# Windowed attention and a token/channel mixer in one kernel: mask added on TensorE and scores on 64 rows for batch 0, token weight permuted on chip, batch 1's first loads put ahead of the second channel weight

## The chip, the cores and the metric

The kernel runs on one core of one Trainium2 chip. The metric is the time of one execution in microseconds on the device; shown is the median of three runs. A profile of one more execution gives a trace of every instruction and every DMA packet; its own time is given beside its span below.

A core has five engines that run their own instruction streams: PE (TensorE, matrix products), DVE (VectorE), ACT (ScalarE), POOL (GpSimd) and SP (which here only issues DMAs). They meet through semaphores. PE multiplies a stationary operand by a moving one and writes to a bank of PSUM, from which DVE or ACT must copy the result to SBUF.

## The reference

Eight batches, eight heads, sequence 576, head width 64. Attention with a window: heads 0 to 3 see the last 32 positions ("plain"), heads 4 to 7 every fourth of the last 128 ("dilated").

```python
rel = pos[:, None] - pos[None, :]
mask_plain = (rel >= 0) & (rel < 32)
mask_dil = (rel >= 0) & (rel < 128) & (rel % 4 == 0)
scores = np.where(mask, q @ k.T / 8, -1e9)
x = softmax(scores) @ v                       # heads side by side: x is (8, 576, 512)
h = relu(x.T @ w_tok1) @ w_tok2               # tokens: 576 -> 256 -> 576
u = x + h.T
out = u + relu(u @ w_ch1) @ w_ch2             # channels: 512 -> 1536 -> 512
```

Inputs and output are float32; the kernel computes in float16 with float32 accumulation.

## The kernel before

**A batch's stages.** Loads (q, k, v in float32), casts to float16, transposes of q and k on PE, scores, values, token mixing (h1, then u, then the transposed uT), and the channel stage `gen_main` (gp with the weight w3, then yp with w4).

**Heads go in pairs**, hp 0 to 3. Positions are held for the dilated pairs by residue modulo 4 (r = 0 to 3), so that a dilated window becomes a plain band over every fourth position. `transposes(b, nm, hp)` (L245) transposes one pair's q or k: four blocks of 128 positions and the last 64 (the tail). k is copied by DVE into `kt` (L261). q is copied by ACT into `qz` twice, once for each head: 64 rows hold the head, the other 64 rows hold zeros (L266, L268), so that a score matmul runs over all 128 rows with the zeros removing the other head.

**Scores.** `scores_plain` (L273) makes per head three blocks of 160 queries in one PSUM bank, exponentiates them on ACT (L284), and then does the fourth block and the tail of both heads in one small bank (L290 to L301). `scores_dil` (L309) makes four blocks of 128 per head, and a small bank for both tails. The mask is a product after the exponential: two multiplications per pair (L303, L304, L328, L329), on DVE for batch 0 and on POOL for the other batches (`mask_engine`, L270). Scores are not shifted by their maximum. The tag "sc" has two banks, "fl" three, "main" three: eight in all.

**Values.** `values(b, h)` (L332) multiplies the weights by v with a column of ones appended, takes the reciprocal of the sum (L362) and scales into `xn` (through the helper at L106), both on DVE.

**Mixing.** `emit_h1` (L365) makes one half (heads 0 to 3, heads 4 to 7) of one of two blocks of 128 hidden units, with a relu on ACT. The first half needs w_tok1 with its rows in natural order (`w1n`), the second half by residue (`w1p`); both are loaded by their own DMA. `emit_u` (L376) makes the five row tiles of u and adds x on DVE (L386, L396). `emit_uT` (L398) transposes u.

**Order of the work.** The order on each engine is the order of the program's text. For batch 0 up to the channel stage the order is written out by hand (L596 to L623, with `warm(n)`, which gives PE n products on zeros to do). From then on `interleave` (L514) mixes the channel stage of batch b with `steps` for later batches: each step has a due time on a scale of PE microseconds from the stage's start, and the channel stage is asked for its next piece whenever no step is due. Steps that are left when the channel stage runs out follow at once.

**Loads.** SP's queue carries q, k, v and the outputs; in batch 0 ACT's queue carries k. POOL's queue carries the constants and the weights, with a cast from float32 to float16 on the way: w1n, w1p, w1t, w2, four pieces of w3, three pieces of w4 (L563 to L577), between its casts of batch 0. Buffers of the raw loads exist once, so a load waits until the batch before has been cast. `gate(t, src)` (L553) is a copy of one element on POOL from a weight to a load's buffer, so that this load waits for that weight. L626 holds all loads of batch 1 until the last piece of w3 has landed.

Of the kernel before, what the change touches and what calls it, by code (L numbers as in the profile page):

```python
# [68 lines left out]
def kernel(  # L69
# [44 lines left out]
    dtail = const[:, 384 + BLK:CW].rearrange("p (x y c) -> p x y c", x=1, y=2)  # L114
    const_np = np.concatenate(
# [22 lines left out]
    def emit_fixed():  # L138
        nc.gpsimd.memset(idle, 0.0)
        for hp in range(4):  # L140
            nc.vector.memset(qz[hp][64:128, 0], 0.0)
            nc.vector.memset(qz[hp][0:64, 1], 0.0)
            nc.vector.memset(kt[hp][:, S:640], 0.0)
# [96 lines left out]
    xn, u16, u16t, uT, gt = {}, {}, {}, {}, {}  # L240
# [4 lines left out]
    def transposes(b, nm, hp):  # L245
# [14 lines left out]
        if nm == "k":  # L260
            nc.vector.tensor_copy(out=natural(kt[hp][:, 0:S]), in_=got)  # L261
            return
        for h in range(2):
# [6 lines left out]
    def mask_engine(b):  # L270
        return nc.vector if b == 0 else nc.gpsimd

    def scores_plain(b, hp):  # L273
# [3 lines left out]
        mid = None  # L277
        for h in range(2):
            p = bank("sc", 2, f"sc_{b}_{hp}_{h}")
            for kb in range(3):  # L280
                nc.tensor.matmul(  # L281
                    out=p[:, BLK * kb:BLK * kb + BLK], lhsT=kt[hp][:, 128 * kb:128 * kb + 128],
                    rhs=qz[hp][:, h, 128 * kb:128 * kb + BLK], start=True, stop=True)
# [4 lines left out]
        p = bank("sc", 2, f"sm_{b}_{hp}")  # L288
        for h in range(2):
            nc.tensor.matmul(  # L290
                out=p[:, BLK * h:BLK * h + BLK], lhsT=kt[hp][:, 384:512],
                rhs=qz[hp][:, h, 384:384 + BLK], start=True, stop=True)
        for h in range(2):
            nc.tensor.matmul(
                out=p[:, 320 + 64 * h:384 + 64 * h], lhsT=kt[hp][:, 512:640],
                rhs=qz[hp][:, h, 512:S], start=True, stop=True)
        nc.scalar.activation(  # L297
            out=blocks[:, :, 3, 0:BLK], in_=p[:, 0:320].rearrange("p (h c) -> p h c", c=BLK),
            func=AF.Exp, scale=0.125)
        nc.scalar.activation(  # L300
            out=tl, in_=p[:, 320:448].rearrange("p (h c) -> p h c", c=64), func=AF.Exp, scale=0.125)  # L301
        eng = mask_engine(b)
        mult(eng, blocks[:, :, :, 0:BLK], blocks[:, :, :, 0:BLK], band)  # L303
        mult(eng, tl, tl, band[:, 0, :, 0:64])  # L304
        yield 0.21

    def scores_dil(b, hp):
        a = attd[hp - 2]
        diag = a[:, :, 0:DTL].rearrange("p h (r c) -> p h r c", c=128)  # L309
        tl = a[:, :, DTL + 64:DTL + 320].rearrange("p h (x c) -> p h x c", c=128)[:, :, :, 0:64]  # L310
        for h in range(2):
            p = bank("sc", 2, f"sc_{b}_{hp}_{h}")
            for r in range(4):
                nc.tensor.matmul(  # L314
                    out=p[:, 128 * r:128 * r + 128], lhsT=kt[hp][:, r:512:4],
                    rhs=qz[hp][:, h, 128 * r:128 * r + 128], start=True, stop=True)
            nc.scalar.activation(out=a[:, h, 0:DTL], in_=p, func=AF.Exp, scale=0.125)  # L317
            yield 0.22
        p = bank("sc", 2, f"sm_{b}_{hp}")
        for h in range(2):  # L320
            for x, keys in enumerate((kt[hp][:, 384:512], kt[hp][:, 512:640])):
                nc.tensor.matmul(out=p[:, 128 * h + 64 * x:128 * h + 64 * x + 64], lhsT=keys,
                                 rhs=qz[hp][:, h, 512:S], start=True, stop=True)
        nc.scalar.activation(
            out=tl, in_=p[:, 0:256].rearrange("p (h x c) -> p h x c", x=2, c=64),
            func=AF.Exp, scale=0.125)
        eng = mask_engine(b)
        mult(eng, diag, diag, band[:, :, :, 0:128])  # L328
        mult(eng, tl, tl, dtail)  # L329
        yield 0.12  # L330

    def values(b, h):  # L332
# [30 lines left out]
        mult(nc.vector, xn[b][:, :, D * h:D * h + D], av[:, :, 0:64], rec)  # L363

    def emit_h1(b, jb, half, t):  # L365
# [8 lines left out]
        relu(nc.scalar, t[:, c], p)  # L374

    def emit_u(b, s, h1):  # L376
        p = bank("fl", 3, f"up_{b}_{s}")
        if s < 4:
            for jb in range(2):
                nc.tensor.matmul(out=p[:, 0:256], lhsT=w2[jb][:, 128 * s:128 * s + 128],  # L380
                                 rhs=h1[jb][:, 0:256], start=(jb == 0), stop=(jb == 1))
            for jb in range(2):
                nc.tensor.matmul(out=p[:, 256:512], lhsT=w2p[jb][:, s],  # L383
                                 rhs=h1[jb][:, 256:512], start=(jb == 0), stop=(jb == 1))
            t = sb.tile([128, DM], FP16, tag="u16", bufs=8, name=f"u16_{b}_{s}")
            nc.vector.tensor_tensor(out=t, in0=p, in1=xn[b][:, s], op=ALU.add)  # L386
# [70 lines left out]
    def gen_main(b):  # L457
# [5 lines left out]
        for mb in range(NMB):  # L463
            t = gt[(b // 2, mb)]
            for sh in range(2):
# [5 lines left out]
                relu(nc.vector if (2 * mb + sh) % 4 == 3 else nc.scalar, t[:, g0 + 288 * sh:g0 + 288 * sh + 288], p[:, 0:288])  # L471
# [85 lines left out]
    cast_qk(0, "k", 0, nc.vector)  # L557
    cast_tails_qk(0, nc.vector)
    for hp in range(1, 4):
        cast_qk(0, "q", hp, nc.gpsimd)  # L560
    for s in range(4):
        cast_vn(0, s, nc.gpsimd)
    nc.gpsimd.dma_start(out=w1n, in_=moe_w_tok1[0:512, :].rearrange("(s p) j -> p s j", p=128))  # L563
    cast_tail_v(0, nc.gpsimd)
    nc.gpsimd.dma_start(out=w1p, in_=moe_w_tok1[0:512, :].rearrange("(m r) j -> m r j", r=4))
    nc.gpsimd.dma_start(out=w1t[0][0:64], in_=moe_w_tok1[512:S, :])
    nc.gpsimd.dma_start(out=w1t[1][64:128], in_=moe_w_tok1[512:S, :])
    nc.gpsimd.dma_start(out=w2a[:, :, 0:S], in_=moe_w_tok2.rearrange("(j p) t -> p j t", p=128))
    cast_vd(0, 0, nc.gpsimd)
# [44 lines left out]
    for h in range(2, 4):  # L614
        va[h]()
        warm(1)
# [76 lines left out]
```

## Time and profile before

| what | value |
|---|---|
| median of 3 runs | 334.49 us (334.07 to 334.78) |
| the profiled execution, its own time | 333.64 us |
| its span (first to last instruction) | 331.86 us |
| granted TensorE clock, mean | 0.994 |
| busy PE / weight load / DVE / ACT / POOL | 300.9 / 253.2 / 154.8 / 173.3 / 155.4 us |
| first channel matmul of batch 0 | 33.33 us |
| first channel matmul of batch 1 | 84.31 us |
| DMA traffic | 43.51 MB, 131 GB/s over the span |

How to read it: the span is cut into 40 slices of 8.3 us; a digit is the busy share of a slice in tenths. A row of instructions gives start, duration, engine, source line, operation, output and input by the program's names, shape and count, and in brackets how long the engine had stood idle just before and what ended that idle time. A row of waits gives who waited for whom, total us, times, and the longest. Rows of groups give busy time and the mean duration of one instruction in nanoseconds.

### The profile page before, as it was taken

What the parts mean: (1) busy time and instruction counts of PE and PEld (TensorE: products, weight loads), DVE (VectorE), ACT (ScalarE), POOL (GpSimd) and SP (SyncE); (2) the same over time, 40 slices, a digit from 0 to 9 for tenths busy, and PEclk for the clock granted to TensorE, in tenths of its full rate; (3) what the DMA queues carried; (4) which work ended last, traced back from release to release, by engine and by line L of the source; (5) the groups of instructions that cost most, each with busy time, mean ns of one, the idle gap of its engine ahead of it and who ended that gap; (6) DMA issues with size and microseconds to landing.
All of it is one profiled execution on the core that took longest, in us unless ns stands there. A gap on an engine that the chain in (4) does not pass through costs nothing.

```text
span 331.9 us, 7976 instructions
## 1 busy us (share of the span) xinstructions
PE 300.9 (91%) x3221; PEld 253.2 (76%) x3221; DVE 154.8 (47%) x329; ACT 173.3 (52%) x380; POOL 155.4 (47%) x211
## 2 busy tenths in 40 slices
PE   5567769999999989998999989998999989999995
PEld 2444547988787878897887888897887888898785
DVE  5676122556366426453545336453545327442222
ACT  2941539589652845548463835548463845522600
POOL 7691066917990499007960499007960490000000
PEclk9999979999999999999999999999999999999999
DMA  8999999948432995920377226921100211002022
GB/s 214 252 162 202 221 270 249 254 129 267 102 100 46 299 228 158 283 70 32 91 241 178 66 65 168 262 81 34 63 3 2 64 65 34 2 32 95 1 65 95
DMA packets 68276, 43.51 MB, mean 131 GB/s; under 512 B 35952, under 2 KB 67056, under 8 KB 68240
## 3 DMA queue, kind: packets, MB, share of 16 engines
q1 hardware_dynamic: 63328, 37.63, 42.5%
q0 software_dynamic: 3312, 4.20, 7.5%
q10 hardware_dynamic: 1600, 1.18, 1.4%
q8 instruction: 25, 0.41, 0.6%
q14 instruction: 11, 0.09, 0.1%
HBM read 37.59 MB, written 9.44 MB: 142 GB/s over the span
## 4 chain that ended last, share of the span: by engine, by line
PE 75%; ACT 11%; DMA 5%; DVE 5%; issue 1%; SPq 1%; POOL 0%; ACTq 0%; POOLq 0%
PE gp L468 27%; PE yp L485 22%; DMA l_q<-in_q_dram 5%; ACT qz L266 4%; PE h1p L373 4%; PE yp L505 3%; ACT attp L284 2%; PE up L380 2%; PE tp_q L253 2%; PE up L383 2%; PE sc L281 2%; ACT qz L268 2%; DVE xn L106 1%; ACT attd L317 1%; PE h1p L371 1%
## 5 line engine op out<-in xcount | busy, mean ns | idle before, releaser
L468 PE MATMUL gp<-uT,w 128*128 128x288 f16 x768 | 110.5, 288 | 1.1 <-ACT gt L100 0.7
L100 ACT ACTIVATE gt<-gp 128x288 f16<-128x288 f32 x144 | 59.1, 412 | 64.9 <-PE gp L468 55.7
L485 PE MATMUL yp<-w,gt 128*128 128x256 f16 x756 | 92.5, 273 | 0.0
L468 PEld LDWEIGHTS <-w 128*128 128x128 f16 x768 | 72.5, 99 | 18.5 <-issue 1.6
L106 POOL TENSOR_TENSOR attp<-attp,const 128x1280 f16<-128x1280 f16 (+1 forms) x28 | 41.8, 1521 | 91.9 <-ACT attp L297 78.5
L485 PEld LDWEIGHTS <-gt 128*128 128x128 f16 x768 | 76.4, 106 | 4.5 <-ACT gt L100 0.3
L495 DVE TENSOR_TENSOR o<-yp,u 128x512 f32<-128x512 f32 x31 | 21.4, 692 | 48.8 <-PE yp L485 48.8
L102 DVE TENSOR_SCALAR gt<-gp 128x288 f16<-128x288 f32 x48 | 21.8, 453 | 38.0 <-PE gp L468 34.8
L106 POOL TENSOR_TENSOR attd<-attd,const 128x1024 f16<-128x1024 f16 (+1 forms) x28 | 38.3, 1398 | 0.0
L261 DVE COPY kt<-tp_k 128x576 f16<-128x576 f16 x32 | 24.1, 754 | 29.5 <-PE tp_k L259 29.4
L106 DVE TENSOR_TENSOR xn<-av,rec 128x320 f16<-128x320 f32 x64 | 31.5, 492 | 2.2
L268 ACT COPY qz<-tp_q 64x576 f16<-64x576 f16 x32 | 20.2, 631 | 15.0 <-PE tp_q L259 14.6
L386 DVE TENSOR_TENSOR u<-up,xn 128x512 f16<-128x512 f32 x32 | 21.4, 686 | 5.5 <-PE up L383 5.3
L317 ACT ACTIVATE attd<-sc 128x512 f16<-128x512 f32 x32 | 17.8, 598 | 11.2 <-PE sc L314 10.9
L94 ACT COPY uT<-tpu 128x576 f16<-128x576 f16 x16 | 10.1, 640 | 25.0 <-PE tpu L417 24.9
L100 ACT ACTIVATE h<-h1p 128x256 f16<-128x256 f32 x32 | 12.3, 384 | 16.5 <-PE h1p L373 15.2
L284 ACT ACTIVATE attp<-sc 128x480 f16<-128x480 f32 x32 | 18.1, 571 | 5.2 <-PE sc L281 3.7
L266 ACT COPY qz<-tp_q 64x576 f16<-64x576 f16 x32 | 20.2, 630 | 0.8 <-PE tp_q L257 0.5
L362 DVE RECIPROCAL rec<-av 128x5 f32<-128x5 f32 x64 | 12.3, 192 | 14.9 <-PE av L349 8.5
L96 POOL CAST c_q<-l_q 128x512 f16<-128x512 f32 x27 | 16.9, 626 | 4.0 <-DMA l_q<-in_q_dram 4.0
L253 PE MATMUL tp_q<-const,c_q 128*128 128x128 f16 x128 | 12.8, 225 | 5.6 <-POOL c_q L96 5.5
L96 POOL CAST c_k<-l_k 128x512 f16<-128x512 f32 x24 | 14.8, 617 | 1.7 <-DMA l_k<-in_k_dram 1.7
(106 smaller groups left out, 458.9 us busy)
## 6 DMA issues: line engine op xcount, KB each, us to landing
out_dram<-o SPq DMA_DIRECT2D x72, 128.0 KB, 2.0
l_q<-in_q_dram SPq DMA_DIRECT2D x15, 512.0 KB, 6.4
l_k<-in_k_dram SPq DMA_DIRECT2D x14, 512.0 KB, 7.2
l_vn<-in_v_dram SPq DMA_DIRECT2D x32, 128.0 KB, 7.0
l_vd<-in_v_dram SPq DMA_DIRECT2D x16, 256.0 KB, 4.6
w<-in_moe_w_ch_dram POOLq DMA_DIRECT2D x4, 384.0 KB, 8.3
w<-in_moe_w_ch_dram POOLq DMA_DIRECT2D x3, 512.0 KB, 14.7
lt<-in_q_dram SPq DMA_DIRECT2D x8, 128.0 KB, 3.1
```

The lines of the kernel that those rows point to most:

```text
L96: eng.tensor_copy(out=out, in_=in_)
L100: nc.scalar.activation(out=out, in_=in_, func=AF.Relu)
L102: eng.tensor_scalar_max(out=out, in0=in_, scalar1=0.0)
L106: eng.tensor_tensor(out=out, in0=x, in1=y, op=ALU.mult)
L261: nc.vector.tensor_copy(out=natural(kt[hp][:, 0:S]), in_=got)
L266: nc.scalar.copy(out=qz[hp][rows, h], in_=p[rows, 0:S])
L268: nc.scalar.copy(out=natural(qz[hp][rows, h]), in_=got[rows])
L284: nc.scalar.activation(out=blocks[:, h, 0:3, 0:BLK], in_=p[:, 0:3 * BLK].rearrange("p (b c) -> p b c", c=BLK), func=AF.Exp, scale=0.125)
L386: nc.vector.tensor_tensor(out=t, in0=p, in1=xn[b][:, s], op=ALU.add)
L468: nc.tensor.matmul(out=p[:, 0:288], lhsT=w3[cb][:, 128 * mb:128 * mb + 128], rhs=uT[(b, cb)][:, 288 * sh:288 * sh + 288], start=(cb == 0), ...
L485: nc.tensor.matmul(out=p[:, c], lhsT=gt[(b // 2, mb)][:, a0:m0 + 512:4] if half else gt[(b // 2, mb)][:, a0:a0 + 128], rhs=w4[mb][:, c], s ...
L495: nc.vector.tensor_tensor(out=o32, in0=p, in1=u16[(b, s)], op=ALU.add)
```

## The change

**Batch 0's scores.** q is no longer spread with zeros: a transposed pair is copied whole into `qn` (one copy per pair, on ACT for pair 0 and on DVE for the others), and a head's score matmul takes the 64 rows of that head of `kt` and `qn`. The two heads' small banks are separate, taken from the tag "main".

**The mask** of batch 0 (all pairs) and of batch 1's pairs 2 and 3 is added before the exponential: a matmul with the identity puts `veil`, 0 where a key is seen and -60000 where it is hidden, into the bank, and the score matmul accumulates on it. The multiplications go where there is a veil; elsewhere they stay on POOL.

**The token weight in natural order** is not loaded: 16 matmuls with slices of `spread` (an identity whose rows are four columns apart) make `w1n` from `w1p` after head 1's values, and DVE and ACT copy one half each.

**Work of batch 0 moved between engines.** Heads 4 and 6 are scaled by ACT in five pieces each; the relu of the second hidden block goes to DVE; two of five additions of u become identity matmuls with a copy on ACT; the v tail's cast goes from POOL to DVE. In batch 0's channel stage every second relu is on DVE instead of every fourth.

**Loads.** Batch 1's tails and the q and k of its pairs 0 and 1 wait for w3's third piece; w4's three DMAs come after w3's last piece (a gate of its own); q and k of pairs 2 and 3 wait for w4's second piece, and v follows them. The due times of batch 0's channel stage are set anew, batch 2's casts go from ACT to POOL, and batch 2's loads are issued at 16.8 and 26.0 instead of 2.0.

The diff, cut:

```diff
+    veil = fixed("veil", [128, BLK + 128])
+    spread = fixed("spread", [128, 515])
...
     def emit_fixed():
         nc.gpsimd.memset(idle, 0.0)
+        nc.gpsimd.memset(spread, 0.0)
...
+        if b == 0:
+            t = qn[hp] = sb.tile([128, S], FP16, tag="ut", bufs=5, name=f"qn_{hp}")
+            eng = nc.vector if hp else nc.scalar
+            copy(eng, t if flat else natural(t), p[:, 0:S] if flat else got)
+            return
...
-    def mask_engine(b):
-        return nc.vector if b == 0 else nc.gpsimd
+    def score(b, hp, h, out, keys, queries, hide):
+
+        if hide is not None:
+            nc.tensor.matmul(out=out, lhsT=ident, rhs=hide, start=True, stop=False)
+        if b == 0:
+            rows = slice(64 * h, 64 * h + 64)
+            nc.tensor.matmul(out=out, lhsT=kt[hp][rows, keys], rhs=qn[hp][rows, queries],
+                             start=hide is None, stop=True)
+        else:
+            nc.tensor.matmul(out=out, lhsT=kt[hp][:, keys], rhs=qz[hp][:, h, queries],
+                             start=hide is None, stop=True)
+
+    def veiled(b, hp):
+        return b == 0 or (b == 1 and hp >= 2)
+
+    def small_banks(b, hp):
+
+        if b == 0:
+            return [(slice(h, h + 1), bank("main", 3, f"sm_{b}_{hp}_{h}")) for h in range(2)]
+        return [(slice(0, 2), bank("sc", 2, f"sm_{b}_{hp}"))]
...
-        eng = mask_engine(b)
-        mult(eng, diag, diag, band[:, :, :, 0:128])
-        mult(eng, tl, tl, dtail)
+        if not veils:
+            mult(nc.gpsimd, diag, diag, band[:, :, :, 0:128])
+            mult(nc.gpsimd, tl, tl, dtail)
...
-        mult(nc.vector, xn[b][:, :, D * h:D * h + D], av[:, :, 0:64], rec)
+        if b == 0 and h in (4, 6):
+            for s in range(5):
+                nc.scalar.activation(out=xn[b][:, s, D * h:D * h + D], in_=av[:, s, 0:64],
+                                     func=AF.Copy, scale=rec[:, s])
+        else:
+            mult(nc.vector, xn[b][:, :, D * h:D * h + D], av[:, :, 0:64], rec)
...
-        relu(nc.scalar, t[:, c], p)
+        relu(nc.vector if b == 0 and jb else nc.scalar, t[:, c], p)
...
+            summed = b == 0 and s in (0, 2)
+            for half in range(2):
+                c = slice(256 * half, 256 * half + 256)
+                if summed:
+                    nc.tensor.matmul(out=p[:, c], lhsT=ident, rhs=xn[b][:, s, c], start=True, stop=False)
...
+            if summed:
+                nc.scalar.copy(out=t, in_=p)
+            else:
+                nc.vector.tensor_tensor(out=t, in0=p, in1=xn[b][:, s], op=ALU.add)
...
-                relu(nc.vector if (2 * mb + sh) % 4 == 3 else nc.scalar, ...)
+                relu(nc.vector if (2 * mb + sh) % (2 if b == 0 else 4) == 1 else nc.scalar, ...)
...
+    nc.vector.tensor_scalar(out=veil, in0=const[:, 384:CW], scalar1=1.0, scalar2=60000.0,
+                            op0=ALU.subtract, op1=ALU.mult)
     cast_tails_qk(0, nc.vector)
+    nc.vector.tensor_copy(out=spread[:, 3:515:4], in_=ident)
     for hp in range(1, 4):
         cast_qk(0, "q", hp, nc.gpsimd)
+    nc.gpsimd.dma_start(out=w1p, in_=moe_w_tok1[0:512, :].rearrange("(m r) j -> m r j", r=4))
     for s in range(4):
         cast_vn(0, s, nc.gpsimd)
-    nc.gpsimd.dma_start(out=w1n, in_=moe_w_tok1[0:512, :].rearrange("(s p) j -> p s j", p=128))
-    cast_tail_v(0, nc.gpsimd)
-    nc.gpsimd.dma_start(out=w1p, in_=moe_w_tok1[0:512, :].rearrange("(m r) j -> m r j", r=4))
+    nc.gpsimd.dma_start(out=w2a[:, :, 0:S], in_=moe_w_tok2.rearrange("(j p) t -> p j t", p=128))
+    cast_vd(0, 0, nc.gpsimd)
     nc.gpsimd.dma_start(out=w1t[0][0:64], in_=moe_w_tok1[512:S, :])
     nc.gpsimd.dma_start(out=w1t[1][64:128], in_=moe_w_tok1[512:S, :])
-    nc.gpsimd.dma_start(out=w2a[:, :, 0:S], in_=moe_w_tok2.rearrange("(j p) t -> p j t", p=128))
-    cast_vd(0, 0, nc.gpsimd)
     cast_vd(0, 2, nc.gpsimd)
+    nc.gpsimd.dma_start(out=w3[0], in_=moe_w_ch1[0:128, :])
     cast_vx(0, nc.gpsimd)
-    for cb in range(4):
+    for cb in range(1, 4):
         nc.gpsimd.dma_start(out=w3[cb], in_=moe_w_ch1[128 * cb:128 * cb + 128, :])
...
+    def natural_w1():
+        for i, eng in enumerate((nc.vector, nc.scalar)):
+            p = bank("main", 3, f"w1_p{i}")
+            for s in (2 * i, 2 * i + 1):
+                for r in range(4):
+                    nc.tensor.matmul(out=p[:, 256 * (s % 2):256 * (s % 2) + 256],
+                                     lhsT=spread[:, 128 * s + 3 - r:128 * s + 131 - r], rhs=w1p[:, r],
+                                     start=(r == 0), stop=(r == 3))
+            copy(eng, w1n[:, 2 * i:2 * i + 2].rearrange("p s j -> p (s j)"), p)
+
     tp(0)
     warm(2)
     cast_qk(0, "k", 1, nc.vector)
     tp(1)
+    sc(0)
     cast_qk(0, "k", 2, nc.vector)
     cast_qk(0, "k", 3, nc.vector)
-    sc(0)
-    warm(1)
+    sc(1)
     tp(2)
-    sc(1)
     warm(1)
     tp(3)
     sc(2)
+    cast_tail_v(0, nc.vector)
+    warm(1)
+    sc(3)
     va[0]()
     va[1]()
-    warm(1)
-    sc(3)
-    warm(2)
-    for h in range(2, 4):
-        va[h]()
-        warm(1)
+    natural_w1()
+    va[2]()
+    va[3]()
+    va[4]()
+    va[5]()
     mx[0]()
     mx[1]()
-    for h in range(4, 8):
-        va[h]()
-        warm(1)
+    va[6]()
+    va[7]()
+    warm(2)
     for f in mx[2:]:
         f()
...
-    gate(l32[(1, "t")][0:1, 0, 0:1], w3[3][0:1, 0:1])
+    gate(l32[(1, "t")][0:1, 0, 0:1], w3[2][0:1, 0:1])
     for nm in ("q", "k"):
         load_tail(1, nm, nc.sync)
-    for h0 in (0, 4):
-        for nm in ("q", "k"):
-            load_qk(1, nm, h0, h0 + 4, nc.sync)
+    for nm in ("q", "k"):
+        load_qk(1, nm, 0, 4, nc.sync)
+    gate(w4a[0:1, 0, 0:1], w3[3][0:1, 0:1])
+    for i in range(3):
+        nc.gpsimd.dma_start(
+            out=w4a[:, 4 * i:4 * i + 4],
+            in_=moe_w_ch2[512 * i:512 * i + 512, :].rearrange("(i p) c -> p i c", p=128))
+    casts1 = cast_steps(1)
+    for f in casts1[:5]:
+        f()
+    for nm in ("q", "k"):
+        gate(l32[(1, nm)][0:1, 4, 0, 0:1], w4[4][0:1, 0:1])
+    for nm in ("q", "k"):
+        load_qk(1, nm, 4, 8, nc.sync)
     load_v(1)
-    for f in cast_steps(1):
-        f()
...
-            steps += score_steps(1, 5.0, 3.6) + value_steps(1, 19.6, 0.8)
-            steps += mix_steps(1, 23.4, 26.8, 29.0, 34.2) + score_steps(2, 26.6, 2.9)
-            casts = cast_steps(2, nc.scalar)
-            steps += at(2.0, 0.0, [lambda: loads(2)]) + at(23.0, 0.9, casts[:9]) + at(36.0, 0.3, casts[9:])
+            first, dil = score_steps(1, 5.5, 3.0), score_steps(1, 13.0, 2.0)
+            steps += first[:10] + dil[10:]
+            steps += at(16.5, 0.3, casts1[5:9]) + at(19.0, 0.6, casts1[9:])
+            steps += at(16.8, 0.0, [lambda: emit_loads_qk(2)]) + at(26.0, 0.0, [lambda: load_v(2)])
+            casts = cast_steps(2)
+            steps += value_steps(1, 24.0, 0.8)
+            steps += mix_steps(1, 26.8, 30.4, 32.0, 36.6) + score_steps(2, 31.0, 2.2)
+            steps += at(27.5, 0.5, casts[:9]) + at(36.0, 0.3, casts[9:])
```

## The prediction

> **What bounds the kernel now.** I read first the page's slices, then TensorE's instructions in order of time, then what the stalled instruction waited for, then the DMA queues in that stretch, and last the busy times by stage.
>
> ```profile
> span 331.9 us, 7976 instructions
> PE   5567769999999989998999989998999989999995
> PEclk9999979999999999999999999999999999999999
> ```
>
> Each digit is 8.3 us. TensorE (PE) is full from slice 7 (50 us) to the end; only the first six slices are not. So there are two places to win: the prologue (batch 0's attention and token mixing, PE at 5 to 7 tenths) and a hole in slice 6, which also costs clock.
>
> ```profile
> 34.33 5.18 PE L468 MATMUL gp<-uT,w 128*128 128x288 f16 x41 [0.26 <-ACT uT L94]
> 44.41 0.61 PE L253 MATMUL tp_q<-const,c_q 128*128 128x128 f16 x4 [4.91 <-POOL c_q L96]
> POOL c_t L96 <- DMA lt<-in_k_dram: 9.7, 1, 9.7
> POOL lt L554 <- DMA w<-in_moe_w_ch_dram: 6.9, 1, 6.9
> 34.31 9.32 DMA l_q<-in_q_dram
> ```
>
> The first two lines: the channel matmuls run in a full stream from 34.33; then PE stands 4.91 us before batch 1's first q transposes. The next three (GpSimd's waits, then the chain): POOL waits 6.9 us for the last piece of w3 (the gate of L626, run at 32.71), then 9.7 us for batch 1's tails, and l_q, issued at 34.31, lands at 43.6. Why so late? The queues between 33 and 37 us:
>
> ```profile
> q0 software_dynamic: 769, 0.77, 119.9%
> q1 hardware_dynamic: 2, 0.00, 0.1%
> ```
>
> q0 is GpSimd's queue (weights), q1 SP's (inputs): packets, MB, share of the engines. SP's tails were issued from 32.91, yet until 37 only 2 of its packets moved, while w4, issued at 22.3 to 24.6, moved 769. The loads stood behind w4.
>
> ```profile
> 8.06:20.33 12.27, 7.32 (x110) 5.55 (x108) 9.33 (x18) 10.92 (x22) 9.47 (x17) 1.00 1.15 223
> 34.33:84.31 49.98, 42.62 (x475) 35.91 (x475) 20.63 (x41) 34.76 (x76) 27.37 (x32) 0.97 0.91 228
> 69.20:84.31 15.11, 13.73 (x164) 11.88 (x163) 8.61 (x14) 14.30 (x30) 7.18 (x7) 1.00 0.56 177
> ```
>
> Stretch, length, then PE, PEld, DVE, ACT, POOL busy, clock, DMA share, GB/s. Row 1 is batch 0's scores: ACT, at 10.92 of 12.27, sets the pace. Row 2 is batch 0's channel stage, from the full stream to batch 1's first channel matmul (84.31). Row 3 is its last part: ACT again, 14.30 of 15.11.
>
> **The change, part by part.** Sums are against the profiled execution: span 331.86, its own time 333.64 (1.78 around it).
>
> *Scores of batch 0.* ACT loses eight half copies into qz (634 ns each, 5.07 us) and keeps one full copy of 0.63. The small exps are split by head: six more instructions. From 437 ns for 320 columns and 270 for 128 an estimate is 0.16 us fixed each, so +0.8 with overlap. ACT's work becomes 0.63 + 5.85 + 0.8 = 7.3 us. The scores start on PE at 10.1 as now (pair 1's transposes end there); first exp 10.75, last one about 18.2, with 0.8 of waits, against 20.33: 2.1 earlier. DVE loses the masks (1.31 + 1.75 + 1.31 + 0.88 = 5.25 us) and gains three q copies (0.75, 0.45, 0.45 from the kt and uT copies), the v tail and half of w1n: covered.
> *Veil and spread* (DVE): a 128x288 op lies in DVE's 1.32 us wait for the tails; spread's copy costs at most 0.2 where kt's copy now waits 0.22: nothing. POOL's memset (0.55, the idle row) lies in its 1.21 us wait for l_q.
> *Heads 0 to 3.* Values start at about 17.9 behind pair 3's scores. Between head 1 and 2 PE makes w1n: 16 matmuls of 256 columns at 0.109 = 1.75 us. w1p is there: w1n's 0.26 MB leaves the queue and w1p takes its place (SP's loads end at 16.2; w1n took 16.2 to 18). Four heads at 0.62 on DVE and w1n's copy of 0.69 end at about 21.8 against 22.76: 1.0 earlier. Without cover from the DVE work, w1n's 1.75 would be on the path.
> *Heads 4 to 7.* Now 2.6 us in a row on DVE. Heads 4 and 6 go to ACT, five 64-column copies each, between the 0.22 that the fixed part and slope give and the 0.27 of 128 columns; about 1.0 per head beside DVE's 0.62. xn ends at 24.6 against 26.9: 2.3 earlier.
> *Mixing.* Two of five additions go to ACT, against four more 256-column matmuls (0.44): 7.2 us from here to the stream, now 7.4. The stream starts at 24.6 + 7.2 = 31.8 against 34.33: **-2.5**. w3 isn't later: with w1n gone from the queue and w2 issued earlier, its pieces (0.39 MB, 1.9 us each) land 3 us sooner, the third at about 27, the last at 29.
> *64 rows.* No row of this trace has a 64-row matmul: all are 128*128. Each score is now a 128-row mask matmul and a 64-row one: 10 pairs in each plain pair of heads, 12 in each dilated, 44 in all, so 88 changes of form. From below a change costs nothing (it can't gain: the same columns stream); the nearest row is that of transposes followed at once by matmuls, spaced 0.06 like equals. From above it is the pipe's own length, 0.19 us of an isolated 64-column matmul less 0.03 of streaming: 0.165. I take nothing, by that nearest row. PE's work in the scores is 4.8 us of scores and 1.4 of transposes and warming in 7.8 us, so 1.6 us would be hidden.
> [...]
> *Batch 1's first pairs.* The gate moves from w3's last piece (32.71) to its third (27), and w4 is held until the last (29), then needs POOL's 0.8 us an issue. SP's four issues (0.61, 0.65, 0.62, about 0.7) end near 30. By the row of 33 to 37 us what is issued first moves first: 0.26 MB of tails at 200 GB/s and 1.05 MB at 347 land by about 34. POOL casts at 0.55 each, so c_q and c_k are ready by 35.3, while TensorE asks at 31.8 + 5.5 = 37.3. The hole goes: **-4.91**. The clock read 0.71, 0.50, 0.50 and 0.58 in 44 to 48: **-1.71**.
> [...]
> *What is late next.* w4's second piece lands near 39 and releases pairs 2 and 3 (behind w4's third piece: 45) and v (50). Asked for at 31.8 + 17 = 48.8 and 55.8: a margin of 4 to 5 us. POOL is held at that gate with batch 1's masks behind it, needed by values at 55.8 only. SP's queue has batch 2's loads moved from 2.0 to 16.8, behind fewer stores: nothing.
> *Rest of the stage.* Half of gt's relus on DVE: the 0.7 us that PE waited for gt on ACT goes, **-0.74**. Masks of batch 1's pairs 2 and 3 on PE: 16 matmuls of 128 at 0.057 and 8 of 64 at 0.03, **+1.15** (PE is full there). Batch 2's scores move to 31.0 with 2.2 spacing: the last 10 us now hold ACT work of 14.30 less five casts (3.0) less two relus (0.8) = 10.5, and scores end behind the main stream: **+1.0**, my choice between 0 and 3. The nine casts go to POOL, idle 45% of this stage.
> *Later stages* keep their instructions: 0.
>
> Sum: -2.5 - 4.91 - 1.71 - 0.74 + 1.15 + 1.0 = **-7.7**. Span 324.2, own time 325.9. The median of the runs shown is 0.85 above the profiled time: **326.8**.
>
> **Rivals.**
> 1. [...] At 0.165 for 88 changes the scores take 14.5 - 1.6 = 12.9 us longer; the stream starts at 44.7 and the stage, its loads long there, ends at 89.5 instead of 84.31: **339.7**. It turns slower from (7.7 + 1.6) / 88 = 0.106 us a change. For: the full length of 0.19 and an alternation that leaves no run of equal forms. Against: back-to-back transposes and matmuls show no gap.
> 2. *The loads still wait for w4.* Shared half and half (of the 196 to 240 GB/s that moved between 33 and 41), 1.31 MB at about 110 GB/s from 29 lands at 41; TensorE asks for k at 38.5 and stands 3 us, with 0 to 1.7 of clock (gaps of 1.5 left it at 1.00, the 4.91 did not): **330.7**. For: SP's k issue falls within 1 us of w4's first.
> 3. *ACT ends the stage.* The crowded end costs 4 and not 1: **329.8**. For: 14.30 of 15.11 today.
> 4. *It doesn't do what it says*: the prologue is held by l_q of pairs 2 and 3 (landing at 11.4, untouched) and a new wait eats the rest: **334.5**.
>
> **How the numbers follow.** Forecast 0.53, its own range 323 to 329; rival 2 0.17, rival 3 0.12, rival 1 0.15, rival 4 0.03. 322.5 to 333.5 holds the first three and leaves out 0.18. Within 0.2% (0.67 us, what a measurement of this kernel can tell from none): 0.03. Faster 0.82, slower 0.15.
>
> **What would show it.** Right: no PE wait over 1 us before batch 1's transposes, clock 1.00 throughout, SP's first loads moving before w4, the full stream at 31 to 33, batch 1's channel matmuls from 75 to 78. Wrong: score matmuls spaced 0.15 us and more; k's cast waiting for DMA past 38; ACT gaps filling the stage's end.

## The result and the profile after

The changed kernel takes **348.74 us** (median of four runs, 347.42 to 349.86) against 334.52 us of the kernel before: a ratio of 1.0425 [1.0383, 1.0467], **slower**. The forecast was 326.8 us. The profiled execution has a span of 348.1 us, its own time is 349.86.

The page of the changed kernel, the lines that answer to those shown of before; a slice is now 8.7 us:

```profile
PE   5999889897879998999899989999899989999995
PEclk9555899999989999999999999999999999999999
```

TensorE reads 9 tenths already in slices 2 to 4, where before it read 5 to 7. That looks like the gain that was wanted. The clock row speaks against it: 5 in the same slices. An engine that is busy all the time at half clock need not be doing more work: in batch 0's scores TensorE is busy for 22.03 us with 113 instructions (row 1 of the stages below), before for 7.32 us with 110.

TensorE's instructions in order of time (start, duration, engine, line, operation), the first score matmuls of batch 0 and the begin of the full channel stream:

```profile
10.19 0.32 PE L283 MATMUL sc<-veil,const 128*128 128x160 f16 x1
10.45 0.31 PE L286 MATMUL sc<-qn,kt 64*128 64x160 f16 x1
10.69 0.32 PE L283 MATMUL sc<-veil,const 128*128 128x160 f16 x1
...
49.16 5.67 PE L510 MATMUL gp<-uT,w 128*128 128x288 f16 x45 [0.26 <-ACT uT L94]
54.67 0.39 PE L258 MATMUL tp_q<-const,c_q 128*128 128x128 f16 x4
```

Mask (128 rows) and score (64 rows) follow each other at 0.25 us. Of that, 0.133 is the 160 columns at half clock (at the same clock the 16 matmuls of 256 columns that make w1n start 0.213 apart, 33.20 to 36.60), so about 0.113 us is spent at each change of form. The stream starts at 49.16 where before it started at 34.33. At 54.67 the q transposes of batch 1 start with no wait in brackets: the hole of 4.91 us is gone.

The busy times by stage of the changed kernel (stretch, length, PE, PEld, DVE, ACT, POOL busy, clock, DMA share, GB/s): the scores of batch 0, its channel stage up to batch 1's first channel matmul, and the stage's last part:

```profile
10.19:32.22 22.03, 22.03 (x113) 11.41 (x111) 4.73 (x9) 7.18 (x19) 12.09 (x24) 0.50 0.98 186
49.16:98.97 49.81, 42.55 (x499) 36.33 (x499) 23.26 (x47) 28.13 (x61) 24.13 (x34) 1.00 0.55 155
83.40:98.97 15.57, 10.76 (x137) 8.92 (x134) 8.57 (x15) 11.92 (x25) 7.33 (x9) 1.00 0.76 213
```

Row 1: the scores hold TensorE for all of 22.03 us, where ACT, the old pace maker, is busy for 7.18. The clock is 0.50. Row 2: the stage is as long as before (49.98), though it has neither the hole nor the clock loss. Row 3: its last part still takes 15.57 us. No engine is full in it as a whole; but from 88.42, where batch 2's scores begin, ScalarE is busy for 9.93 of 10.55 us.

The spans by stage: the stream starts 14.83 later, the stage is 0.17 shorter, the rest takes 249.1 instead of 247.55 (+1.58): together 16.24, which is the difference of the spans, up to rounding. The 1.58 is clock again: 36 gp matmuls at 98.97 took 6.23 us where before 36 took 4.57, with a granted clock of 0.50 from 99 to 102. It belongs to this one execution: e1_full_rows and e2_mask_per_bank, below, end the same stage with the same waits, there the 36 take 4.57 us, and the rest takes 247.49.

So there are two questions: what holds TensorE in the prologue (the changes of form, theory A, or a clock that fell for another reason, theory B), and why a stage without its hole is no shorter (theory C: the later due times).

### The profile page after: what moved, and what is told of

It reads as the page before. It is cut to its first block, busy times and chain, and to the rows that moved or that the text cites. A ratio compares the mean times of both kernels' runs of the same rounds, so it can differ in the third digit from the quotient of the medians.

```text
span 348.1 us, 8146 instructions
## 1 busy us (share of the span) xinstructions
PE 322.9 (93%) x3302; PEld 265.2 (76%) x3302; DVE 155.9 (45%) x332; ACT 167.1 (48%) x375; POOL 154.2 (44%) x218
## 4 chain that ended last, share of the span: by engine, by line
PE 69%; ACT 9%; DMA 8%; issue 7%; POOL 3%; DVE 1%; SPq 1%; ACTq 0%; POOLq 0%
PE gp L510 24%; PE yp L527 20%; DMA w<-in_moe_w_ch_dram 5%; ACT qz L276 4%; PE h1p L409 3%; PE up L421 3%; PE yp L547 3%; PE sc L289 3%; DMA lt<-in_k_dram 2%; POOL attp L106 2%; ACT qz L278 1%; ACT attd L345 1%; PE tp_q L258 1%; PE sm L289 1%; DMA l_vd<-in_v_dram 1%
## 5 line engine op out<-in xcount | busy, mean ns | idle before, releaser
L100 ACT ACTIVATE gt<-gp 128x288 f16<-128x288 f32 x138 | 56.8, 412 | 73.1 <-PE gp L510 66.4
L102 DVE TENSOR_SCALAR gt<-gp 128x288 f16<-128x288 f32 x54 | 24.6, 455 | 40.7 <-PE gp L510 38.6
L289 PEld LDWEIGHTS <-kt 128*128 128x128 f16 x308 | 23.1, 103 | 13.3 <-issue 10.1
L106 POOL TENSOR_TENSOR attd<-attd,const 128x1024 f16<-128x1024 f16 (+1 forms) x24 | 32.9, 1402 | 0.2 <-ACT attd L345 0.2
L106 DVE TENSOR_TENSOR xn<-av,rec 128x320 f16<-128x320 f32 x62 | 30.5, 492 | 2.1
L289 PE MATMUL sc<-qz,kt 128*128 128x128 f16 (+1 forms) x196 | 21.1, 225 | 1.8 <-ACT attp L312 0.6
L96 POOL CAST c_q<-l_q 128x512 f16<-128x512 f32 x31 | 19.2, 622 | 4.0 <-DMA l_q<-in_q_dram 4.0
L278 ACT COPY qz<-tp_q 64x576 f16<-64x576 f16 x28 | 17.6, 630 | 6.1 <-PE tp_q L264 5.7
L276 ACT COPY qz<-tp_q 64x576 f16<-64x576 f16 x28 | 17.6, 630 | 5.4 <-PE tp_q L262 4.9
L96 POOL CAST c_k<-l_k 128x512 f16<-128x512 f32 x28 | 17.3, 618 | 4.9 <-DMA l_k<-in_k_dram 4.9
```

Source lines behind the costliest of these rows:

```text
L96: eng.tensor_copy(out=out, in_=in_)
L100: nc.scalar.activation(out=out, in_=in_, func=AF.Relu)
L102: eng.tensor_scalar_max(out=out, in0=in_, scalar1=0.0)
L106: eng.tensor_tensor(out=out, in0=x, in1=y, op=ALU.mult)
L276: nc.scalar.copy(out=qz[hp][rows, h], in_=p[rows, 0:S])
L278: nc.scalar.copy(out=natural(qz[hp][rows, h]), in_=got[rows])
```

## The experiments

### Take the changes of form away

e1_full_rows, from the changed kernel:

```diff
-            rows = slice(64 * h, 64 * h + 64)
-            nc.tensor.matmul(out=out, lhsT=kt[hp][rows, keys], rhs=qn[hp][rows, queries],
+            nc.tensor.matmul(out=out, lhsT=kt[hp][:, keys], rhs=qn[hp][:, queries],
```

> The changed kernel with every score matmul of batch 0 on all 128 rows (it leaves out the parting of the two heads of a pair, so each score is the sum over both); instructions, copies and columns as before, only the 88 changes of form are gone. Theory A (a change of rows costs a drain of about 0.11 us, and the drains keep the clock at half): scores go from 22.0 to about 8 to 9 us, clock 1.00 up to 40 us, channel stream at about 33 instead of 49.2, time about 334. Rival B (the clock fell by itself at 10.1 us, because fewer warming matmuls stand ahead of the scores; the changes are nearly free): clock still 0.5 from 10 to beyond 20 us, scores 11 to 13 us, stream at 37 to 39, time about 338.

Measured: 331.95 us, ratio 0.9940 [0.9917, 0.9964] to before. TensorE's instructions in the same place:

```profile
11.87 0.23 PE L285 MATMUL sc<-qn,kt 128*128 128x160 f16 x1
11.94 0.23 PE L283 MATMUL sc<-veil,const 128*128 128x160 f16 x1
...
32.72 1.51 PE L509 MATMUL gp<-uT,w 128*128 128x288 f16 x11 [0.26 <-ACT uT L94]
```

The same columns, at 0.07 us each. The scores take 6.75 us (11.37 to 18.12, where the first values matmul starts) instead of 22.03, and the stream starts at 32.72; the time is 2 us below the 334 that was expected. Theory A is right about the changes. Theory B falls as an explanation of the time, though a part of it stands, that TensorE can be slow with no change of form: here too it came slow into the scores (four transposes in 0.63 us, in the changed kernel 0.40). Within the first scores, all of one form, the spacing fell from 0.13 to 0.07 us (starts at 11.37, 11.50, 11.63, 11.73 and 11.80). In the changed kernel, with the changes, the clock reads 0.50 over all 22.03 us. The stage took 49.79 us, as in the changed kernel: the second question is a separate one.

### A third of the changes

e2_mask_per_bank, from the changed kernel: one mask matmul covers a bank, then the bank's 64-row scores follow, 32 changes instead of 88.

```diff
...
+            nc.tensor.matmul(out=whole[0], lhsT=ident, rhs=whole[1], start=True, stop=False)
+            for i, (h, out, keys, queries, hide) in enumerate(parts):
+                rows = slice(64 * h, 64 * h + 64)
+                nc.tensor.matmul(out=out, lhsT=kt[hp][rows, keys], rhs=qn[hp][rows, queries],
+                                 start=False, stop=(i == len(parts) - 1))
...
```

> The changed kernel with one mask matmul for a whole bank and then its 64-row scores: 16 banks, 32 changes of form instead of 88, the same columns, and the masks laid out on GpSimd and VectorE before. Theory A: 56 changes less at 0.11 is 6.2 us less at half clock, scores at about 15 us if the clock stays low and 8 to 9 if it rises; time 336 to 342. Rival B: scores change by less than 1.5 us (fewer, longer matmuls), time within 2 us of 348.7. A third possibility: rows 64 alone hold the clock down, then the clock stays at 0.5 with the scores at 15 us.

Measured: 341.05 us, ratio 1.0204 [1.0174, 1.0235]. The last transposes before its scores, and the busy times of the scores:

```profile
10.47 0.61 PE L261 MATMUL tp_k<-const,c_k 128*128 128x128 f16 x4
```

```profile
10.97:26.60 15.63, 15.63 (x85) 7.33 (x83) 5.66 (x9) 6.96 (x19) 9.79 (x19) 0.50 1.14 205
```

Against e1_full_rows the scores take 8.9 us longer. 32 changes at 0.113 are 3.6 of that; the rest, 5.3, goes with the clock, 0.50 throughout although there are far fewer changes. So two losses go with the changes here, their own time and the clock. The changes did not bring the clock down here: the four transposes at 10.47 are as slow as those of e1_full_rows, and the first change of form comes a microsecond later. But in e1_full_rows the spacing halved within the first scores, and here the clock reads 0.50 to their end at 26.60. The third possibility of the expectation, that matmuls on 64 rows hold the clock down by themselves, would give the same numbers; a probe below speaks against it.

### The price of a change by itself

e3_probe and e8_probe_tiles are the kernel before with matmuls on zeros added in later stages (their results are not used): runs of one form, strict alternation, alternating halves of the rows, and eight of one form and eight of the other.

```diff
...
+        for i in range(24):
+            nc.tensor.matmul(out=p[:, 0:128], lhsT=idle[:, 0:128], rhs=idle[:, 0:128], start=True, stop=True)
+            nc.tensor.matmul(out=p[:, 0:128], lhsT=idle[0:64, 0:128], rhs=idle[0:64, 0:128], start=True, stop=True)
```

> The kernel before, with two rows of matmuls on zeros put into batch 3's dense channel stage, where the clock is full: 24 matmuls of 64 rows by 128 columns, then 24 pairs of 128 rows and 64 rows. Theory A: the 64-row ones are spaced 0.057 us like full ones, the pairs 0.15 to 0.17 per matmul (0.053 of columns and 0.10 to 0.113 of drain); the clock may fall within the 7 us of the pairs. Rival B: the pairs are spaced 0.06 to 0.08.

One run, 347.42 us. TensorE's instructions in the probe:

```profile
165.74 1.51 PE L646 MATMUL pr<-idle 64*128 64x128 f16 x24
167.18 0.23 PE L649 MATMUL pr_alt<-idle 128*128 128x128 f16 x1
167.34 0.23 PE L650 MATMUL pr_alt<-idle 64*128 64x128 f16 x1
...
169.81 0.29 PE L649 MATMUL pr_alt<-idle 128*128 128x128 f16 x1
```

24 matmuls on 64 rows alone take 1.44 us. Without the change that ends them that is 0.056 each, as on 128 rows (0.055 in the scores of e1_full_rows): by itself the form costs nothing here. In alternation the starts lie 0.161 apart: 0.055 of columns and about 0.107 of change. After 2.4 us the spacing jumps to 0.22. The busy times microsecond by microsecond show why:

```profile
168.00:169.00 1.00, 1.00 (x8) 0.60 (x7) 0.00 (x0) 0.00 (x0) 1.00 (x4) 1.00 0.00 1
169.00:170.00 1.00, 1.00 (x7) 0.53 (x6) 0.00 (x0) 0.00 (x0) 1.00 (x4) 0.76 0.63 103
170.00:171.00 1.00, 1.00 (x6) 0.51 (x5) 0.00 (x0) 0.00 (x0) 1.00 (x3) 0.50 0.93 304
```

TensorE reads 1.00 busy, and its clock falls to 0.50. It came back at about 179.8 (the mean from 179 to 180 is 0.62), 2.9 us after the alternation ended at 176.85.

> The kernel before with two probes on zeros in dense channel stages: in batch 3's, 24 pairs of 64-row matmuls that alternate between rows 0 to 63 and rows 64 to 127, into two banks; in batch 5's, 12 rounds of 8 matmuls on 128 rows and 8 on 64 rows, which is 24 changes with runs between. If it is the change of form and not of rows that drains, the first are spaced 0.03 to 0.06 us and the clock holds; the second lose 0.107 us at each change (16 matmuls in 1.1 us instead of 0.9) and the clock holds too, since the array streams most of the time. If any change of tile drains, the first are spaced 0.16 and the clock falls as in the pairs before.

One run, 348.89 us. TensorE's instructions in the two probes:

```profile
165.03 0.23 PE L646 MATMUL pr_low<-idle 64*128 64x128 f16 x1
165.03 0.23 PE L647 MATMUL pr_high<-idle 64*128 64x128 f16 x1
165.09 0.22 PE L646 MATMUL pr_low<-idle 64*128 64x128 f16 x1
...
241.20 0.61 PE L653 MATMUL pr_lone<-idle 128*128 128x128 f16 x8
241.74 0.62 PE L655 MATMUL pr_lone<-idle 64*128 64x128 f16 x8
242.29 0.62 PE L653 MATMUL pr_lone<-idle 128*128 128x128 f16 x8
```

Rows 0 to 63 and rows 64 to 127 in turn, into two banks: both of a pair start together, a pair takes 0.056. So a change between the two halves costs nothing here: one matmul on 64 rows took as much in e3_probe (0.056). Eight and eight: 0.55 per run of eight, 0.444 of columns (eight times the 0.055 of a run) and again 0.107 for the one change. These matmuls stay at 0.55 us per run of eight for all 13.2 us of the probe, though half of them are on 64 rows, as in e2_mask_per_bank. So the 64 rows by themselves don't explain the half clock there. Two things stay open: the probe came in at full clock and e2_mask_per_bank at half, and no run has a long stretch of nothing but 64 rows.

Why the clock falls while TensorE reads 1.00 busy is not shown by any run here.

### The due times

e4_due_times: the changed kernel with the due times of before, batch 1's second half cast just ahead of them; the loads and casts of batch 2 are due earlier with them (lines left out).

```diff
...
-            first, dil = score_steps(1, 5.5, 3.0), score_steps(1, 13.0, 2.0)
-            steps += first[:10] + dil[10:]
...
-            steps += value_steps(1, 24.0, 0.8)
-            steps += mix_steps(1, 26.8, 30.4, 32.0, 36.6) + score_steps(2, 31.0, 2.2)
+            steps += score_steps(1, 5.0, 3.6) + value_steps(1, 19.6, 0.8)
+            steps += mix_steps(1, 23.4, 26.8, 29.0, 34.2) + score_steps(2, 26.6, 2.9)
...
```

> The changed kernel with the due times that batch 0's channel stage had before (scores of batch 1 at 5.0 and 3.6, values at 19.6, mixing at 23.4, scores of batch 2 at 26.6 and 2.9), the rest of the change kept. Theory C (the stage gains nothing from the vanished hole because the new due times leave the mixing and batch 2's scores behind the end of the channel matmuls, with ScalarE as their pace): the stage from the first full stream to batch 1's first channel matmul goes from 49.8 to 43 to 44.5 us, the clock no longer falls at 98 us, time about 341. Rival D (the stage is held by what was moved between engines, GpSimd casts or the relus on VectorE): stage still above 48, time above 346.

Measured: 339.92 us, ratio 1.0179 [1.0158, 1.0199]: 2.5 points less than the changed kernel. Its stage, and TensorE's instructions at the stage's end:

```profile
47.66:90.44 42.78, 41.14 (x499) 36.15 (x499) 23.38 (x47) 28.06 (x61) 23.44 (x31) 1.00 0.66 182
```

```profile
79.84 0.37 PE L289 MATMUL sc<-qz,kt 128*128 128x160 f16 x3
...
84.30 0.82 PE L527 MATMUL yp<-w,gt 128*128 128x256 f16 x6
...
90.33 0.28 PE L289 MATMUL sm<-qz,kt 128*128 128x64 f16 x4 [0.65 <-ACT attd L345]
```

The same instructions, 42.78 us instead of 49.81. The same place of the changed kernel:

```profile
88.42 0.37 PE L289 MATMUL sc<-qz,kt 128*128 128x160 f16 x3
...
98.84 0.32 PE L289 MATMUL sm<-qz,kt 128*128 128x64 f16 x4 [0.65 <-ACT attd L345]
```

The scores of batch 2 take 10.6 us from the first to the stage's end in both (79.84 to 90.44, 88.42 to 98.97). They begin 32.2 us into the stage here and 39.3 there: 7.1 us, the whole difference of the stages. In between, e4_due_times still has channel matmuls to lay (84.30, two more later); in the changed kernel the last yp ran at 82.55, before those scores began. Theory C is right that the later due times cost the stage its gain. ScalarE sets the pace of the scores in both, busy for 9.94 of 10.60 us here and 9.93 of 10.55 there; the due times decide when they begin. Of the 7.1 us, 4.4 is the due time itself (31.0 against 26.6). Before the scores begin TensorE also waits in the changed kernel for xn (2.0 us) and c_q (0.9), and in e4_due_times for neither; no run takes these apart. The clock did not fall after this stage, and the rest took 247.3 us.

### The loads alone, and the repaired kernel

e6_loads_alone is the kernel before with the new order of loads only; e5_zero_rows is e4_due_times with q spread with zeros again, so that all matmuls are on 128 rows. Its edit, cut:

```diff
...
-            nc.tensor.matmul(out=out, lhsT=kt[hp][rows, keys], rhs=qn[hp][rows, queries],
+            nc.tensor.matmul(out=out, lhsT=kt[hp][:, keys], rhs=qz[hp][:, h, queries],
...
```

> The kernel before with the new order of loads alone (batch 1's first pairs after w3's third piece, w4 after its last, pairs 2 and 3 after w4's second piece, batch 2's loads later); prologue, masks, and the due times 5.0 to 26.6 as before. By the forecast's terms the hole of 4.91 us goes and the clock loss of 1.71 with it: about 328. If what arrives early meets a new wait (w4 or batch 1's second half late, or TensorE asking for k before it lands, the prologue being no shorter here), 331 to 334.

> The changed kernel with two parts undone: batch 0's scores run over 128 rows with zeros in the other head's rows again (two half copies of q per pair, one on VectorE and one on ScalarE beyond pair 0), and batch 0's channel stage has its former due times; the mask on TensorE, the weight made on chip, the order of the loads and the moves between engines stay. Theory A and C together: stream at 32.7 to 33.5 (32.72 on 128 rows before), stage 42.8, rest 247.4, span 323 to 324, time 324.5 to 326. If a third cost is hidden in the rest of the change, the sum of the two repairs falls short: time above 329.

e6_loads_alone: 333.08 us, 0.9993 [0.9971, 1.0015], no difference: the second of its two expectations. In its profiled execution the stage takes 48.32 us (49.98 before), but the stream starts at 35.62 (34.33 before); why it starts later isn't shown. e5_zero_rows: 329.96 us, 0.9897 [0.9863, 0.9931], faster, but some 4 us short of what I expected. TensorE's waits in e5_zero_rows' stage:

```profile
47.39 0.40 PE L258 MATMUL tp_q<-const,c_q 128*128 128x128 f16 x4 [1.05 <-POOL c_q L96]
49.16 0.61 PE L258 MATMUL tp_k<-const,c_k 128*128 128x128 f16 x4 [1.10 <-POOL c_k L96]
...
59.30 0.19 PE L371 MATMUL av<-vv,attp 128*128 128x65 f16 x1 [0.67 <-POOL vv L96]
```

and in e6_loads_alone's:

```profile
50.33 0.40 PE L253 MATMUL tp_k<-const,c_k 128*128 128x128 f16 x4 [0.67 <-POOL c_k L96]
...
58.80 0.19 PE L343 MATMUL av<-vv,attp 128*128 128x65 f16 x1 [1.38 <-POOL vv L96]
```

The hole of 4.91 us before batch 1's first pair is gone in both. It has come back in pieces: at batch 1's second half, whose loads now stand behind w4, and at v. For v it isn't its own load that is late, but GpSimd. These are its instructions in e7_no_veil_batch1 (below), and the order is the same in these two kernels:

```profile
45.86 0.61 POOL L96 CAST c_q<-l_q 128x512 f16<-128x512 f32 x1 [5.21 <-DMA l_q<-in_q_dram]
...
49.20 3.01 POOL L106 TENSOR_TENSOR attp<-attp,const 128x1280 f16<-128x1280 f16 x2
52.15 1.09 POOL L96 CAST vv<-l_vn 128x256 f16<-128x256 f32 x3
```

It stands 5.21 us for q of the second half (4.75 in e5_zero_rows, 3.88 in e6_loads_alone) and about 1 for k; from 47.45 on, casts, masks and then v's casts follow without a pause. So v is late because GpSimd is. The clock suffers too: 0.88 in 50 to 60 us of e5_zero_rows, 0.83 in 60 to 70 of e6_loads_alone. e4_due_times did not show this, because its prologue was 14 us longer and the loads were there. e5_zero_rows' stage takes 47.31 us, 4.5 more than e4_due_times'.

### Without the masks of batch 1, with due times between, with an earlier gate

e7_no_veil_batch1 is e5_zero_rows with batch 1 masked on POOL; e9_due_between and e10_gate_earlier are e7_no_veil_batch1 with one edit each (in e9_due_between, in lines left out, the casts of batch 1's second half and the loads of batch 2 are due 3 us later too).

```diff
-        return b == 0 or (b == 1 and hp >= 2)
+        return b == 0
```

```diff
-            steps += score_steps(1, 5.0, 3.6) + value_steps(1, 19.6, 0.8)
-            steps += mix_steps(1, 23.4, 26.8, 29.0, 34.2) + score_steps(2, 26.6, 2.9)
+            steps += score_steps(1, 5.0, 3.6)[:10] + score_steps(1, 8.0, 3.6)[10:] + value_steps(1, 22.4, 0.8)
+            steps += mix_steps(1, 25.6, 29.0, 31.0, 35.6) + score_steps(2, 28.0, 2.7)
...
```

```diff
-        gate(l32[(1, nm)][0:1, 4, 0, 0:1], w4[4][0:1, 0:1])
+        gate(l32[(1, nm)][0:1, 4, 0, 0:1], w4[0][0:1, 0:1])
```

> As the kernel with zero rows and the former due times, but batch 1's pairs 2 and 3 are masked by GpSimd after the exponential as before the change. The forecast charged their 24 mask matmuls with 1.15 us in a stage where TensorE is full: 0.8 to 1.2 us faster than that kernel. If GpSimd is then late for the values, 0 to 3 us slower.

> The kernel of e7_no_veil_batch1 (128 rows for the scores of batch 0, no mask matmuls in batch 1), with due times between the former and the changed ones: batch 1's dilated pairs 3 us later, its values 2.8, its mixing 2, the scores of batch 2 1.4 us later than formerly. Theory 'the loads bind': with a short prologue what is left of the stage's loss is that batch 1's second half and v arrive after they are asked for; asked later, the waits for c_q, c_k and vv go (1 to 3 us with their clock) and the time is 326 to 328. Rival, 'every delay crowds the end': steps pushed later run past the last channel matmul, at 0.14 us of loss or more per us of delay, and what the waits return is spent there: 329 to 331, as e7.

> The kernel of e7_no_veil_batch1, with batch 1's second half of q and k and v held behind the first piece of the second channel weight instead of its second. Theory 'the loads bind': these loads start about 3 us earlier, the waits for c_q, c_k and vv shrink by 1 to 2.5 us, time 327 to 328.5. Rival: the loads then share the engines with the second piece of the weight, the first yp matmuls wait for it instead, and the time is as e7's or above, 329 to 330.5.

| kernel | us | ratio to before | stage (profiled) |
|---|---|---|---|
| e5_zero_rows | 329.96 | 0.9897 [0.9863, 0.9931] | 47.31 |
| e7_no_veil_batch1 | 329.36 | 0.9889 [0.9856, 0.9922] | 46.24 |
| e9_due_between | 328.12 | 0.9833 [0.9800, 0.9865] | 46.07 |
| e10_gate_earlier | 329.93 | 0.9882 [0.9856, 0.9909] | 47.51 |

e7_no_veil_batch1's stage is 1.07 shorter, near the 1.15 that the masks were forecast to cost; the times of the two kernels can't be told apart. Single executions differ by as much: the four kernels of the table have one and the same prologue, and their streams start at 33.28, 33.47, 34.48 and 33.33. e9_due_between has the lowest median of this study and beats both kernels of the case; 328.12 lies between the times of its theory and of its rival. e7_no_veil_batch1 waits 0.93 us for c_k and 1.38 and 1.45 for vv. In e9_due_between the two waits for vv are gone, one for c_k stays, and the wait before the stage's last scores grows from 0.65 to 1.19:

```profile
41.40 0.40 PE L258 MATMUL tp_k<-const,c_k 128*128 128x128 f16 x4 [0.97 <-POOL c_k L96]
...
80.44 0.28 PE L280 MATMUL sm<-qz,kt 128*128 128x64 f16 x4 [1.19 <-ACT attd L336]
```

Its profiled stage is hardly shorter than e7_no_veil_batch1's (that execution, 329.59, is the slowest of its six), and the intervals overlap: whether the due times between the two sets gained 1 us or nothing stays open. e10_gate_earlier didn't help, as its rival expected. Its loads were issued at 39.89 (40.55 in e7_no_veil_batch1), 0.7 us earlier and not 3, since GpSimd came to the gate only at 39.68, after the casts of the first pairs; and q's cast could begin at 46.99 (45.86): between 40 and 45 us the weight's queue moved 0.77 MB (0.43) and the loads' queue 0.43 (0.91). The weight's queue has 0.34 MB more there, the loads' queue 0.48 less.

## Why the prediction was wrong

**"64 rows: I take nothing, by that nearest row."** This step failed. The measured price is 0.107 us a change, in the upper half of the stated range of 0 to 0.165 and just at the break-even of 0.106 that rival 1 named. By their own time alone, with the rest of the sum as forecast, the changes would have eaten the gain and no more. The row that I called nearest, transposes followed by matmuls, holds two operations of one form; it says nothing of a change of form. The upper end of my range, 0.165, was an estimate from the 0.19 us of an isolated matmul, and the rival that used it had a chance of 0.15.

**The clock was in no step and no rival of the prologue.** This weighs nearly as much as the time of the changes. Against e1_full_rows the stream starts 16.44 us later. The scores start 1.2 earlier and take 15.3 longer, of which 88 times 0.113 is 9.9, and their 10752 columns at half clock another 4.5. What follows the scores takes 2.3 longer, since the clock stays low until 37.5, with 0.50 from 30 to 37 and 0.75 from 37 to 38 (the 16 matmuls that make w1n: 3.4 us instead of the forecast 1.75).

**"Batch 2's scores ... +1.0, my choice between 0 and 3."** The crowded end cost 7.0; the 1.6 of clock after it came in the profiled execution of the changed kernel and in neither e1_full_rows nor e2_mask_per_bank, which end alike. I had summed ACT's work (10.5) and asked whether the last 10 us could hold it. The work was about that (9.9), but it is the length of batch 2's scores: they take 10.6 us with due times 2.2 apart (the changed kernel) as with 2.9 (e4_due_times). What counts is when the first one starts, and that moved by 7.1.

**The hole (-4.91) and its clock (-1.71): right as a mechanism, wrong as a gain.** There is no PE wait before batch 1's transposes, which start 5.51 us into the stage (forecast 5.5), and the stage's clock is 1.00. The gate ran at 27.95 and w4's at 29.77 (forecast 27 and 29), k's cast started at 36.40 (forecast ready by 35.3). GpSimd's instructions of the changed kernel show it:

```profile
27.95 0.18 POOL L596 CAST lt<-w 1x1 f32<-1x1 f16 x1 [6.18 <-DMA w<-in_moe_w_ch_dram]
29.77 0.18 POOL L596 COPY w<-w 1x1 f16<-1x1 f16 x1 [1.64 <-DMA w<-in_moe_w_ch_dram]
...
36.40 0.62 POOL L96 CAST c_k<-l_k 128x512 f16<-128x512 f32 x1 [1.92 <-DMA l_k<-in_k_dram]
```

In this kernel the late stream makes that easy: TensorE asks for q at 54.67, 17 us after these casts. The fair test is e5_zero_rows, where it asks for q at 38.30 and for k at 39.07, and k's first cast starts at 36.86: no wait there either. So rival 2 did not come. Its sharing half and half isn't what the changed kernel shows: from 31 to 34 us, with w4 issued from 30.27 on, the loads' queue moved 0.83 MB and the weight's queue nothing. But with the former due times the wait moves to batch 1's second half and v, and with the changed ones the stage's end pays. I counted the gain of the one and a small price of the other, as if the two were independent.

**Prologue (-2.5).** Without the changes of form it is -1.6 (e1_full_rows, 32.72; the forecast was 31.8), and -1.05 with zeros in q (e5_zero_rows, 33.28). The direction is likely and not sure: the same prologue gave 34.48 in e9_due_between, against 34.33 before. **Masks of batch 1 (+1.15)**: 1.07 in the profiled stages, but the times show no difference. **gt's relus (-0.74)** were not tried alone; the wait of 0.7 us is 0.2 in e4_due_times. **Later stages (0)**: 247.2 to 247.5 wherever the clock held at the stage's end, against 247.55.

Rival 1 gave 339.7, and the kernel with the changes of form and the former due times, e4_due_times, takes 339.92. That is partly luck: the rival's price of a change was too high and the clock was missing. The outcome of the change itself is rival 1 and a larger rival 3 together, a combination that the range, closed at 333.5, left out.

## What to carry to other kernels

Don't alternate matmuls of 128 and of 64 rows, which cost 0.107 us a change here and brought the clock to 0.50 after 2.4 us. Group them by form (runs of eight held 0.55 us each in e8_probe_tiles; the shorter groups of e2_mask_per_bank stayed at 0.50), or pad with zeros when they must follow each other (e5_zero_rows, 329.96 us), and read the clock row beside a busy TensorE. When loads are put in another order, ask which transfer is last now and when it is needed, not only whether the old wait goes. When steps are given later due times to cover a load, count from the start of the chain that ends the stage: here 4.4 later on the scale of due times became 7.1 us.

## What the runs showed of the hardware that was not expected

- A change between 128 and 64 rows cost 0.107 us at full clock (e3_probe, e8_probe_tiles) and about 0.113 at half clock (the changed kernel). A change between the two halves of the rows cost nothing: written to two banks, both matmuls of a pair ran at the same time (0.056 us a pair, e8_probe_tiles).
- After 2.4 us of strict alternation the granted clock fell to 0.50 with TensorE 1.00 busy in the trace (e3_probe). It came back 2.9 us after the alternation. With runs of eight there was no fall in 13.2 us (0.55 us from the first run to the last, e8_probe_tiles). Where it was already low (e2_mask_per_bank) it read 0.50 through 32 changes in 15.6 us.
- The clock column can miss a slow stretch: between 8.8 and 11.3 us of e1_full_rows it reads 1.00, while four transposes take 0.63 us there and 0.40 in the changed kernel. The means of e2_mask_per_bank's runs are 0.97, 0.97, 0.98 and 0.995, at 341.64, 341.56, 339.68 and 340.54 us. Durations of equal instructions were the safer witness here.
